# Retention into dropless experts on one core: q scaled ahead of v in two of twelve steps, and the filling counts taken behind the early rows' numbers

## The chip, the cores and the metric

The kernel runs on 1 core of one Trainium2 chip. The metric is device time in microseconds (us) of one launch. Inputs and outputs are float32 in device memory. The core has five engines with a queue of instructions each: TensorE (PE, matrix products), VectorE (DVE), ScalarE (ACT), GpSimd (POOL) and SyncE (SP, which here only starts transfers). They run side by side and wait for each other through semaphores.

## What is computed

Two blocks follow each other. The first is a recurrent retention over 768 positions, for 4 batches and 8 heads of width 64; the second sends each of the 3072 resulting rows (512 wide) to one of 8 experts.

```python
# retention, per batch and head
state = gamma * state + outer(k[t], v[t])
y[t]  = scale * q[t] @ state
# x = y, as 3072 rows of 512
logits = x @ w_gate;  e = argmax(logits);  gate = softmax(logits)[e] / (1 + 1e-9)
out    = gate * (relu(x @ w1[e]) @ w2[e])     # w1[e]: 512x1024, w2[e]: 1024x512
```

Every row goes through exactly one expert, and an expert takes all rows that chose it.

## The kernel before

**Twelve steps of attention.** The recurrence is computed in chunks of 128 positions. A step `s` (0 to 11, `STEPS` is 12) does one chunk for two of the four batches (`b` = 0, 1). `where[s]` is (pair of chunks, pair of batches, which chunk of the pair): steps 8 and 10 begin the last pair of chunks, 9 and 11 end it. For each of its two batches a step does the following:

- `scale_q` (L489) and `scale_v` (L494) multiply q and v by powers of the decay, on POOL. One `scale_v` is one instruction, one `scale_q` is two. The q of two steps are loaded and scaled together, so q of step 10 (as the code counts) serves steps 10 and 11.
- `turn_q` and `turn_k` (L500) transpose q and k on TensorE with an identity into banks of PSUM (`trq`, `trk`), and ACT copies them out.
- `scores` (L532) multiplies k and q into four banks `sc`; DVE masks them (`am`, L536). `with_state` (L555) multiplies q with the old state, `next_state` (L568) makes the new one (`new`) out of k and the scaled v, and DVE adds it to the old one (L574). `within` (L586) multiplies the masked scores with the scaled v, and ACT copies the result `y` out as `x[s]`.
- `logits` (L614, L623) makes the gate's logits of the step before; `to_rows` (L597, DVE) turns its x into rows and `store` (L604, SP) writes them to `x_d` in device memory.

**Where the rows go.** `place(i)` takes the logits of a stretch of steps (0 to 4, 5 to 8, 9 to 11) and numbers the rows of each expert: one-hot `ohs`, ranks by counting products on TensorE (`rk`, L666 to L670), counts per expert in `acc[:, i + 1]`, and through a product `found` (L708) the list `inv` (L712) of which row sits in which place. It is a generator; `WHEN` says at which points of which step its next piece is issued. For the second stretch the last pieces fall into step 10: `found` and then `inv` are issued ahead of `to_rows(9)`, and `next_state(10)` comes behind.

**Early tiles.** After the second stretch the first 256 places of experts 0 and 1 can be fetched before attention ends. `sources` (L184 to L187) makes the row numbers `src_e`, and POOL issues four indirect transfers from `x_d` into `xs` (L173), two for each expert, with the two `scale_v` of step 11 (counted from 0) between them. ACT copies expert 0's rows to `xe` (L768), TensorE transposes them in step 11 (`tre`, L776) between the two halves of `within`, and the first layer of expert 0 (`hp`, L232) follows. `pad_ranks` (L723 to L731) raises the counts of experts 0 and 1 to at least 256, so that later rows take places behind these tiles: TensorE sums the counts of two experts (`tot`, L726), and three small DVE instructions make `pad` and add it to `acc`. Its result is read by `rk` of the last stretch, at 133.53 us.

**What sets the order.** All engines stand under a manual schedule: each runs its instructions in the order in which the code issues them, and SP and POOL likewise. SP issues q, k, v, the rows' stores and the weights in one queue. The lines around the change are these; the first two numbers of a pair in `SCALED` are steps counted from 0:

```python
VALUES = {STEPS - 5: (STEPS - 3, STEPS - 2)}                 # loads: v of 9 and 10 in step 7
SCALED = {STEPS - 4: (STEPS - 4, STEPS - 3), STEPS - 3: (STEPS - 2,), STEPS - 2: ()}
...
if s % 2 and s + 1 < STEPS:
    scale_q(s + 1, 1)
for i in SCALED.get(s, (s,) if 0 < s < STEPS - 1 else ()):
    for b in range(2):
        scale_v(i, b)
if s % 2 == 0 and s + 2 < STEPS:
    scale_q(s + 2, 0)
```

So before, POOL's order from step 8 on is v8, v9, q10 (both batches), v10, two instructions per batch for q and one for v.

**PSUM.** `ps(tag, bufs, name)` hands out banks of a tag in turn. The tag `tr` has two banks, which `trk`, `found`, `tot`, `new`, `rk` and `tre` share; who asks for a bank waits until its last user has read it.

Of the kernel before, what the change touches and what calls it, by code (L numbers as in the profile page):

```python
# [40 lines left out]
def inner(ap, n):  # L41

    dims = [list(d) for d in ap.ap]
    return bass.AP(tensor=ap.tensor, offset=ap.offset, ap=dims + [[0, n]])
# [9 lines left out]
def kernel(  # L54
# [25 lines left out]
    STEPS = NT // 2  # L80
    NEXT = (0, 5, 9, STEPS)
    NR = len(NEXT) - 1
# [7 lines left out]
    def ps(tag, bufs, name):  # L90
        return psum.tile([P, 512], F32, tag=tag, name=name, bufs=bufs)
# [28 lines left out]
    def rt(shape, name, dt=F32):  # L120
        return route.tile(shape, dt, tag=name, name=name)
# [20 lines left out]
    acc = rt([P, NR + 1, E], "acc", BF16)  # L142
# [28 lines left out]
    def gather(xs, idx, tiles, rows=N):  # L171
        for t in tiles:
            nc.gpsimd.indirect_dma_start(  # L173
                out=xs[:, t, :], out_offset=None, in_=x_d[0:rows, :],
                in_offset=bass.IndirectOffsetOnAxis(ap=idx[:, t : t + 1], axis=0), bounds_check=rows - 1,
                oob_is_err=False)
# [3 lines left out]
    def sources(got, name):  # L180
        m = got.shape[2]
        tok, far = rt([P, m], f"tok{name}"), rt([P, m], f"far{name}")
        src = rt([P, m], f"src{name}", U32)
        nc.vector.tensor_scalar(out=far, in0=got[:, 0, :], scalar1=1.0, scalar2=float(FAR), op0=ALU.is_lt, op1=ALU.mult)  # L184
        nc.vector.tensor_tensor(out=far, in0=got[:, 1, :], in1=far, op=ALU.add)
        nc.vector.scalar_tensor_tensor(out=tok, in0=got[:, 0, :], scalar=float(L), in1=far, op0=ALU.mult, op1=ALU.add)
        nc.vector.tensor_scalar(out=src, in0=tok, scalar1=-float(L), scalar2=None, op0=ALU.add)  # L187
        return src, far
# [262 lines left out]
    with ExitStack() as actx:  # L451
# [32 lines left out]
        def scale_q(s, b, by=nc.gpsimd, parts=1):  # L484
            got = raw.pop(("q", s, b))
            qs = raw["qs", s, b] = att.tile([P, 2, H, D], F32, tag="qs", name="qs")
            for part in (ts(i, H // parts) for i in range(parts)):
                for e in range(2):
                    by.tensor_tensor(out=qs[:, e, part, :], in0=got[:, part, ts(e, D)], op=ALU.mult,  # L489
                                     in1=inner(dec[:, ts(2 * where[s][0] + e, H)][:, part], D))  # L490

        def scale_v(s, b, by=nc.gpsimd):
            vs = att.tile([P, H, D], F32, tag="vs", name="vs", bufs=4)
            by.tensor_tensor(out=vs, in0=raw.pop(("v", s, b)), op=ALU.mult,  # L494
                             in1=inner(dec[:, ts(NC + 2 * where[s][0] + where[s][2], H)], D))
            raw["vs", s, b] = vs
# [18 lines left out]
        def turn_k(s, b):  # L515
            kT = att.tile([P, HP, P], F32, tag="kT", name="kT")
            tr = pairs_of("tr", 2, "trk")
            heads_first(raw["k", s, b], tr)
            nc.scalar.copy(out=kT, in_=tr)
            front[s, b] = kT  # L520
# [4 lines left out]
        def scores(s, b):  # L525
            kT, qT = front.pop((s, b)), q_of(s, b)
            sc = [pairs_of("sc", 4, "sc") for _ in range(2)]
            am = [att.tile([P, HP, P], F32, tag=f"am{j}", name=f"am{j}") for j in range(2)]
            for a in range(HP):
                for j in range(2):  # L530
                    r = ts(j, D)
                    nc.tensor.matmul(sc[j][:, a, :], lhsT=kT[r, a, :], rhs=qT[r, a, :], start=True, stop=True)  # L532

            def mask():
                for j in range(2):
                    nc.vector.tensor_tensor(out=am[j], in0=sc[j], in1=middle(causal[:, :], HP), op=ALU.mult)  # L536

            return am, mask
# [3 lines left out]
        def outputs():  # L542
            return [ps("y", 2, "y").rearrange("p (b a t) -> p b a t", b=2, a=HB) for _ in range(2)]
# [86 lines left out]
        def place(i):  # L630
# [82 lines left out]
            if i == NR - 2:  # L713
                head = inv[:, :, 0 : TC + HALF]
                src, far = sources(head, "_e")
                for e in range(2):
                    gather(xs2[e], src[:, e * TC :], range(HALF), 2 * NEXT[i + 1] * P)
                    if e == 0:
                        for b in range(2):
                            scale_v(STEPS - 1, b)  # L720
                early.extend([head, far])

        def pad_ranks(at):  # L723

            tot = ps("tr", 2, "tot")[:, 0:2]
            nc.tensor.matmul(tot, lhsT=ones_b, rhs=at, start=True, stop=True)  # L726
            pad = att.tile([P, 2], F32, tag="pad", name="pad")
            nc.vector.scalar_tensor_tensor(out=pad, in0=inner(row2[:, 0], 2), scalar=float(EARLY), in1=tot,
                                           op0=ALU.add, op1=ALU.subtract)
            nc.vector.tensor_scalar(out=pad, in0=pad, scalar1=0.0, scalar2=2.0, op0=ALU.max, op1=ALU.min)  # L730
            nc.vector.tensor_tensor(out=at, in0=at, in1=pad, op=ALU.add)  # L731

        def load_all(nm, s):
            for b in range(2):
                load(nm, s, b)
# [41 lines left out]
                copies[t](out=xT[:, :, ts(t, P)], in_=tr)  # L777

        VALUES = {STEPS - 5: (STEPS - 3, STEPS - 2)}
        SCALED = {STEPS - 4: (STEPS - 4, STEPS - 3), STEPS - 3: (STEPS - 2,), STEPS - 2: ()}  # L780
        rest = iter(())
        WHEN = {5: "abc", 6: "b", 7: "ab", 8: "pp", 9: "ac", 10: "mpp"}

        def step(s, at):
            for _ in range(WHEN.get(s, "").count(at)):
                next(rest, None)

        for s in range(STEPS):
            if s + 3 < STEPS:
                if s % 2:  # L790
                    load_all("q", s + 3)
                load_all("k", s + 3)
            for i in VALUES.get(s, (s + 2,) if s + 5 < STEPS else ()):
                load_all("v", i)
# [7 lines that stand above are left out]
            if s in (1, 2):  # L802
                nc.gpsimd.memset(xs2[s % 2], 0.0)
            if s:
                am = [scores(s, b) for b in range(2)]
                am[0][1]()
                step(s, "m")
                am[1][1]()
            y = outputs()
            if s + 1 == STEPS:  # L810
                logit = logits(s - 1)
            if where[s][0] or where[s][2]:
                with_state(s, y)

            def ahead():
                for b in range(2):
                    turn_k(s + 1, b)

            def ahead_q():
                if s % 2:  # L820
                    for b in range(2):
                        turn_q(s + 1, b)

            if s:
                if s + 1 < STEPS:
                    logit = logits(s - 1)
                    ahead()
                if s + 1 == STEPS:
                    xe = whole_rows(xs2[0])
                reduce = logits_of(s - 1, *logit)  # L830
                step(s, "p")
                if s + 1 < STEPS:
                    ahead_q()
                to_rows(s - 1)
                reduce()
                if s + 1 == STEPS:
                    wa.append(weights2(first, 0, 2))
                store(s - 1)
                if s == NEXT[NR - 1]:
                    load_all("v", STEPS - 1)  # L840
                    wa = [weights1(first, 0, 2)]
                if s in NEXT:
                    rest = chain(rest, place(NEXT.index(s) - 1))
                step(s, "a")
            next_state(s)
            if s == 0:
                ahead()
            step(s, "b")
            if s == NEXT[NR - 1] + 1:
                pad_ranks(acc[:, NR - 1, 0:2])  # L850
            step(s, "r")
            within(s, y, am, (lambda: early_rows(xe, xTa, (nc.vector.tensor_copy, nc.scalar.copy)))
                   if s + 1 == STEPS else lambda: None)
            step(s, "c")
# [269 lines left out]
```

## Time and profile before

| what | value |
|---|---|
| median of 3 runs | 455.89 us (453.74 to 457.38) |
| the profiled execution's own time | 458.76 us |
| its span, first to last instruction | 456.8 us |
| TensorE busy | 430.3 us, 94% of the span |
| VectorE, POOL, ACT busy | 292.1, 260.5, 131.9 us |
| mean granted TensorE clock | 0.987 of full speed |

The profile is of one execution. Busy times of engines overlap, so they don't add up to the span. "Idle before" a row is the time in which that engine had nothing running, with the event that ended it. Times in the text count from the span's start. Attention takes the first 126 us; the first product of expert 0's first layer starts at 126.13 us, and from there TensorE runs almost without a gap up to the last microseconds.

### The profile page before, as it was taken

What the parts mean: (1) busy time and instruction counts of PE and PEld (TensorE: products, weight loads), DVE (VectorE), ACT (ScalarE), POOL (GpSimd) and SP (SyncE); (2) the same over time, 40 slices, a digit from 0 to 9 for tenths busy, and PEclk for the clock granted to TensorE, in tenths of its full rate; (3) what the DMA queues carried; (4) which work ended last, traced back from release to release, by engine and by line L of the source; (5) the groups of instructions that cost most, each with busy time, mean ns of one, the idle gap of its engine ahead of it and who ended that gap; (6) DMA issues with size and microseconds to landing.
All of it is one profiled execution on the core that took longest, in us unless ns stands there. A gap on an engine that the chain in (4) does not pass through costs nothing.

```text
span 456.8 us, 9680 instructions
## 1 busy us (share of the span) xinstructions
PE 430.3 (94%) x3651; PEld 361.4 (79%) x3651; DVE 292.1 (64%) x600; ACT 131.9 (29%) x298; POOL 260.5 (57%) x216
## 2 busy tenths in 40 slices
PE   6999998969799999999999999999899999999992
PEld 3788887858678868869968985997798689599772
DVE  4454787667868974775776678387677768744410
ACT  2356354334342112310331321124133113202310
POOL 4474544252506978519845890985489189278311
PEclk9999999989899999999999999999999999999997
DMA  8999999999966546644532815172272534001001
GB/s 190 213 236 205 229 205 219 238 214 250 304 187 230 187 120 218 250 187 128 192 99 94 279 53 183 42 292 85 110 249 74 187 101 164 6 5 64 4 29 50
DMA packets 94471, 72.75 MB, mean 159 GB/s; under 512 B 53898, under 2 KB 78474, under 8 KB 94352
## 3 DMA queue, kind: packets, MB, share of 16 engines
q1 hardware_dynamic: 89088, 58.74, 45.9%
q0 software_dynamic: 5120, 12.60, 8.2%
q8 instruction: 47, 0.77, 0.7%
q14 instruction: 72, 0.59, 0.4%
q10 hardware_dynamic: 144, 0.05, 0.0%
HBM read 60.88 MB, written 14.68 MB: 165 GB/s over the span
## 4 chain that ended last, share of the span: by engine, by line
PE 75%; DMA 7%; DVE 7%; issue 4%; SPq 3%; POOL 2%; ACT 1%; POOLq 0%; ACTq 0%; DVEq 0%
PE p L311 27%; PE p L357 17%; PE p L245 13%; DMA q<-in_q_dram 4%; PE hp L232 3%; PE y L586 3%; DMA v<-in_v_dram 3%; SPq L604 2%; PE sc L532 2%; PE p L232 2%; PE new L568 1%; PE y L555 1%; DMA w1t<-in_moe_w_dram 1%; PE yp L357 1%; POOL qs L489 1%
## 5 line engine op out<-in xcount | busy, mean ns | idle before, releaser
L245 PE MATMUL p<-w2t,hT 128*8 128x128 f32 (+6 forms) x496 | 66.4, 360 | 0.0
L245 PEld LDWEIGHTS p<-w2t,hT 128*8 128x8 f32 (+6 forms) x496 | 32.6, 123 | 29.2 <-issue 26.4
L405 POOL DMA_INDIRECT out_dram<-o,dst x30 | 29.9, 995 | 29.1 <-ACT o L253 13.0
L216 DVE STREAM_TRANSPOSE xT<-xs 32x512 f32<-32x512 f32 (+1 forms) x64 | 40.7, 635 | 6.8 <-issue 5.5
L536 DVE TENSOR_TENSOR am<-sc,causal 128x512 f32<-128x512 f32 x48 | 30.0, 683 | 21.0 <-PE sc L532 20.9
L494 POOL TENSOR_TENSOR vs<-v,dec 128x512 f32<-128x512 f32 x23 | 23.7, 1045 | 33.5 <-DMA v<-in_v_dram 33.3
L311 PE MATMUL p<-t,s 128*128 128x196 f32 (+5 forms) x224 | 41.7, 329 | 0.0
L311 PE MATMUL p<-t,w1t 128*128 128x196 f32 (+5 forms) x224 | 41.7, 329 | 0.0
L1083 POOL COPY turn_of<-t 128x1 f32<-128x1 f32 x6 | 1.1, 184 | 70.1 <-DVE t L297 70.1
L315 DVE TENSOR_TENSOR hT<-p,q 128x196 f32<-128x196 f32 (+5 forms) x84 | 28.6, 359 | 16.6 <-PE p L311 16.0
L216 DVE STREAM_TRANSPOSE xTs<-xs 32x512 f32<-32x512 f32 x48 | 33.7, 702 | 7.0 <-issue 6.1
L173 POOL DMA_INDIRECT xs<-x_d,src x28 | 29.6, 1059 | 14.8 <-issue 8.0
L311 PEld LDWEIGHTS p<-t,s 128*128 128x128 f32 x224 | 37.8, 190 | 0.0
L311 PEld LDWEIGHTS p<-t,w1t 128*128 128x128 f32 x224 | 37.8, 190 | 0.0
L357 PE MATMUL p<-ws,hs 128*128 128x256 f32 x168 | 37.4, 379 | 0.0
L315 DVE TENSOR_TENSOR q<-p,q 128x196 f32<-128x196 f32 (+5 forms) x56 | 19.0, 360 | 26.8 <-ACT q L323 13.5
L357 PEld LDWEIGHTS p<-ws,hs 128*128 128x128 f32 x168 | 31.9, 190 | 4.3
L273 POOL TENSOR_TENSOR ws<-w2t,ws 128x1024 f32<-128x1024 f32 x14 | 34.4, 2455 | 0.6
L273 POOL TENSOR_TENSOR ws<-w2t 128x1024 f32<-128x1024 f32 x14 | 33.2, 2369 | 0.1
L489 POOL TENSOR_TENSOR qs<-q,dec 128x512 f32<-128x512 f32 x22 | 22.3, 1042 | 17.0 <-DMA q<-in_q_dram 16.1
L363 DVE SCALAR_TENSOR_TENSOR o<-p,gate,q 128x256 f32<-128x256 f32 x21 | 10.0, 483 | 27.9 <-PE p L357 23.8
L357 PE MATMUL p<-w2t,hT 128*128 128x256 f32 x112 | 26.9, 381 | 0.1
(203 smaller groups left out, 835.1 us busy)
## 6 DMA issues: line engine op xcount, KB each, us to landing
w1t<-in_moe_w_dram SPq DMA_DIRECT2D x7, 2048.0 KB, 8.7
w2t<-in_moe_w_dram SPq DMA_DIRECT2D x7, 2048.0 KB, 9.4
k<-in_k_dram SPq DMA_DIRECT2D x24, 256.0 KB, 5.1
v<-in_v_dram SPq DMA_DIRECT2D x24, 256.0 KB, 5.7
x_d<-xg SPq DMA_DIRECT2D x48, 128.0 KB, 3.9
q<-in_q_dram SPq DMA_DIRECT2D x11, 512.0 KB, 6.1
w1t<-in_moe_w_dram SPq DMA_DIRECT2D x2, 1024.0 KB, 8.6
w2t<-in_moe_w_dram SPq DMA_DIRECT2D x2, 1024.0 KB, 9.8
```

The costliest lines, as they stand in the source:

```text
L173: nc.gpsimd.indirect_dma_start(out=xs[:, t, :], out_offset=None, in_=x_d[0:rows, :], in_offset=bass.IndirectOffsetOnAxis(ap=idx[:, t : t + ...
L216: nc.vector.transpose(xT[ts(g, L), :, 0 : n * P].rearrange("p a (t r i) -> p r t a i", r=Q, i=L)[:, r, :, :, :], xs[ts(r, L), tiles[0] : t ...
L232: nc.tensor.matmul(hp, lhsT=w1t[:, 0, dt, ts(f, P)], rhs=xT[:, dt, 0:n], start=(dt == 0), stop=(dt == DT - 1))
L245: nc.tensor.matmul(y[j * z : j * z + m, 0:c], lhsT=hT[:, f, t * P + r0 : t * P + r0 + m], rhs=w2t[:, 0, f, ts(j, c)], start=(i == 0), stop ...
L273: by.tensor_tensor(out=ws[i], in0=sums[i][0], in1=sums[i][1], op=ALU.subtract)
L311: nc.tensor.matmul(rows(y), lhsT=a(d, f), rhs=b(d), start=start and d == 0, stop=d == 1, skip_group_check=True)
L315: nc.vector.tensor_tensor(out=to, in0=rows(y), in1=rows(plus), op=ALU.add)
L357: nc.tensor.matmul(y, lhsT=a[:, f, :], rhs=b[:, f, :], start=start and f == 0, stop=f == FH - 1, skip_group_check=True)
L405: done = nc.gpsimd.indirect_dma_start(out=out[:, :], out_offset=bass.IndirectOffsetOnAxis(ap=idx[:, t : t + 1], axis=0), in_=o[:, t, :], i ...
L489: by.tensor_tensor(out=qs[:, e, part, :], in0=got[:, part, ts(e, D)], op=ALU.mult, in1=inner(dec[:, ts(2 * where[s][0] + e, H)][:, part], D))
L494: by.tensor_tensor(out=vs, in0=raw.pop(("v", s, b)), op=ALU.mult, in1=inner(dec[:, ts(NC + 2 * where[s][0] + where[s][2], H)], D))
L536: nc.vector.tensor_tensor(out=am[j], in0=sc[j], in1=middle(causal[:, :], HP), op=ALU.mult)
```

## The change

In step 8 POOL scales v of step 8 alone, and v of step 9 moves behind q of step 10, to step 9: POOL's order becomes v8, q10, v9, v10. Counted from one these are the ninth and tenth step. `pad_ranks` is issued inside `place`, behind the early transfers and the two `scale_v` of step 11, instead of behind `next_state(10)`.

```diff
@@ place, for the second stretch
                 for e in range(2):
                     gather(xs2[e], src[:, e * TC :], range(HALF), 2 * NEXT[i + 1] * P)
                     if e == 0:
                         for b in range(2):
                             scale_v(STEPS - 1, b)
+                pad_ranks(acc[:, NR - 1, 0:2])
                 early.extend([head, far])
@@
-        SCALED = {STEPS - 4: (STEPS - 4, STEPS - 3), STEPS - 3: (STEPS - 2,), STEPS - 2: ()}
+        SCALED = {STEPS - 3: (STEPS - 3, STEPS - 2), STEPS - 2: ()}
@@ the loop over steps
             step(s, "b")
-            if s == NEXT[NR - 1] + 1:
-                pad_ranks(acc[:, NR - 1, 0:2])
             step(s, "r")
```

In the compiled program the number of instructions on each engine is the same. On TensorE `tot` goes from behind the 32 products of `new` to ahead of them. On DVE the three instructions of `pad_ranks` go from behind `xg` (two transposes), `lg` and `state` to ahead of them, directly behind `src_e`. On POOL two `vs` go from ahead of four `qs` to behind them. ACT and SP keep their order. As `tot` asks for its bank of `tr` ahead of `new`, `new` gets the bank that `found` held, and in the compiled program its first product then waits for VectorE as well.

## The prediction

> **What bounds the kernel now.** I read the page's slices first, then the waits around the two edits, then the order of time there. TensorE (PE) is busy 94% of the span, and from 126 us on it hardly stops. So what this change can give must come out of the last two steps of attention, 96 to 126 us, and it is worth what it moves the first product of expert 0's first layer (`hp`, L232, 126.13 us) forward.
>
> ```profile
> PE   6999998969799999999999999999899999999992
> PEclk9999999989899999999999999999999999999997
> DMA  8999999999966546644532815172272534001001
> ```
>
> Slices 8 and 10 (91 to 103 and 114 to 126 us) are the only ones ahead of the last where the granted clock dips, and PE has its holes there. DMA is full up to 126 us: transfers set the pace of all that waits for data in this stretch.
>
> ```profile
> 99.78 3.99 PE L500 MATMUL trq<-ident,qs 128*128 128x128 f32 x16 [3.44 <-POOL qs L489]
> 119.52 0.64 PE L614 MATMUL parts<-xT,wg 128*32 128x256 f32 x8 [2.42 <-DVE am L536]
> ```
>
> These are PE's two holes, 5.86 us together. The first ends when POOL has scaled q of step 10 (from 0). POOL's own rows tell why that is late:
>
> ```profile
> 96.65 2.08 POOL L494 TENSOR_TENSOR vs<-v,dec 128x512 f32<-128x512 f32 x2 [10.24 <-DMA v<-in_v_dram]
> 98.69 4.05 POOL L489 TENSOR_TENSOR qs<-q,dec 128x512 f32<-128x512 f32 x4
> 102.69 2.05 POOL L494 TENSOR_TENSOR vs<-v,dec 128x512 f32<-128x512 f32 x2
> ```
>
> POOL stands 10.24 us for v9 with q10 queued behind it, and q10 had landed at 89.8 and 91.7 us (issued at 84.57 and 86.12, median 5.4 to landing). The second hole ends with a mask, and DVE's rows show what held the masks:
>
> ```profile
> 116.17 2.61 DVE L731 TENSOR_TENSOR acc<-acc,pad 128x2 bf16<-128x2 bf16 x1
> 118.70 2.47 DVE L536 TENSOR_TENSOR am<-sc,causal 128x512 f32<-128x512 f32 x4
> ```
>
> Two columns took 2.61 us; the same sum at 106.74 took 0.17. It ends at 118.78, and POOL's two `vs` of step 11 end at 118.74. So a DVE sum of two SBUF operands stood behind POOL's. `scores` were ready at 117.1.
>
> Each hole is paid twice, as the windows show (length, PE busy with its count, the other engines, clock, DMA):
>
> ```profile
> 96.69:100.10 3.41, 0.32 (x3) 0.32 (x4) 3.23 (x6) 0.16 (x1) 3.41 (x4) 1.00 0.93 230
> 100.10:103.51 3.41, 3.27 (x16) 2.29 (x13) 0.71 (x1) 1.84 (x3) 3.41 (x4) 0.50 0.94 224
> 117.17:120.58 3.41, 1.06 (x25) 0.68 (x28) 3.41 (x5) 0.31 (x2) 2.93 (x4) 1.00 0.97 279
> 120.58:123.99 3.41, 3.41 (x42) 2.54 (x34) 2.03 (x4) 1.10 (x3) 0.70 (x1) 0.50 0.93 276
> ```
>
> After a window of 3.41 us with little work, PE runs the next 3.41 us at half clock and loses 1.71. `trq` took 3.99 us for what takes 1.91 at 76.45.
>
> **The order of v and q.** Nothing is added; two `vs` go behind four `qs`. POOL then does q10 from 89.9 (landing) to 92.0 and 92.0 to 94.1, under its old wait. PE's `trq` starts at 96.35 instead of 99.78 and takes 1.75 (chain of waits, full clock) to 98.1. v9 still lands at 96.65, so its `vs` still end at 98.73, then v10 runs to 100.8 (needed by `new` at 108). `within(9)` has 0.25 wait for the second `vs` and ends at 100.1. Next is `rk`, which waits for `ohs` on DVE; `ohs` ends at 100.81 as before, since the DVE chain from 96.96 ran beside POOL work then and does now. PE idles 0.8, `rk` ends at 101.3 (before: 105.94). If the cover of q10 were gone (q landing after v9), the 3.44 would stay.
>
> From there DVE binds: the three gate instructions (0.65) now follow `ohs` at 100.85, `own` starts at 101.55, and after its 1.55 us the masks of step 10 at 103.1, where before they started at 107.60: 4.5 earlier. DVE was full from there to `src_e` (113.82), so `inv` ends at 108.5 and `src_e` at 109.3.
>
> **The counts.** On PE `tot` (0.16) now lies ahead of `new`; harmless itself. But `new` then takes the bank of `found` and waits for `inv`: it starts at 108.6, though PE is through at 107.45 (`found` 111.81 and `tot`, less 4.5). A new wait of 1.15. The queue behind it is `within(10)` and `scores(11)`: `new` 1.10, 1.75, 1.99, so 113.45. On DVE the three `pad` instructions (0.14, 0.17, 0.17 with gaps: 0.6) lie in front of `xg`, `lg`, `state` (2.1), which end at 112.0; the masks of step 11 wait for PE's first eight products (112.5) and not for DVE. POOL's `vs` start at 112.2, long after `acc`. So `parts` runs at 113.45 without a wait, against 119.52: 6.1 earlier. If `acc` is held again, that is a rival below.
>
> **What is late next.** `parts`, `with_state`, the two logit transposes and half of `within` (0.57, 1.03, 0.22, 0.9) end at 116.2. Then `tre` needs `xe`, and that needs the two early transfers of expert 0. POOL issues them 0.29 and 1.85 after `src_e`: 109.6 and 111.15. Stores of rows that they read landed by about 109. Their time to landing:
>
> ```profile
> xs<-x_d,src_e POOLq DMA_INDIRECT x1, 5.1
> ```
>
> ```profile
> xs<-x_d,src_e POOLq DMA_INDIRECT x1, 8.3
> ```
>
> The first is that of 114.11, when most of `w1t` (packets from 110.3 to 117.5) had gone; the second that of 118.91, with all of `w2t` just issued. The four took 5.1, 4.6, 8.3, 8.0. Here a rule speaks: the Trainium skill, page "DMA: Bandwidth & Descriptors", section "Queues, rings and completion order", has each DMA engine go round-robin between queues, packet by packet. By it the transfer needn't wait for the weights: 5.1 and 4.6, landed at 114.7 and 115.8, no wait at `tre`, `hp` at 116.2 + 1.02 + 1.02 = 118.2, a gain of 7.9. By the row of 118.91 the landings are 117.9 and 119.2, `xe` is done at 119.85 (0.6 each), `hp` at 121.5, a gain of 4.6. In the trace the third transfer's packets began only at 123.0, when 269 of `w2t`'s 1024 had started; by then `w1t`, further ahead by 1.2 us, would be at 112.5. I take 1.2 less than the slow row: 7.1 and 6.8, landed at 116.7 and 118.0; `tre` at 117.5 and 118.8 (idle 1.3 and 0.8), then 0.5 and 1.02: `hp` at 120.4. Gain 5.7. Half of `w1t` must have landed (115.95, plus 1.4 for sharing with 0.5 MB): it has.
>
> From `hp` on each transfer is asked for by an instruction that moves along, or has slack (`w2t` landed at 130.35, read at 140.02; expert 1's transfers landed at 128.3, read at 131.24), so the gain reaches the end.
>
> **The sum.** Holes removed 5.86, half clock removed 3.41; new waits 0.25 + 0.8 + 1.15 + 2.1 = 4.3; the remainder to 5.7 (0.7) is rows whose queue gaps I haven't carried. Own time 458.76 becomes 453.1. The runs' median is 2.87 below that execution, and I don't expect all of 5.7 there: the windows above lie on a fixed grid (100.10, 120.58: six times 3.41). The skill's page "TensorE: Matmul & The Clock Gate", "Part 1: The HAM clock gate", calls the window free-running and wants a whole idle window. By that rule the 2.42 hole costs no half clock; the trace has 1.06 of 3.41 busy and half clock after it, so the row decides: somewhere below 2.35 idle is enough. With a threshold of 1.7 to 2.35 and a grid at random, the old holes (3.44, 2.42) cost 1.7 down to 1.0 half-clock windows in a middling run instead of 2: 1.1 us less to win. My new hole at `tre` (2.2 in parts) costs one at most in half of the runs: 0.4. So 5.7 - 1.1 - 0.4 = 4.2, and 455.89 becomes **451.7**.
>
> **Rivals.**
> - *The early transfers land in time* (fast row, 7.9 - 1.1 = 6.8): **449.0**. For it: the round-robin rule; against: the slow rows.
> - *They come late and PE falls to half clock at `tre`* (4.6 - 1.1 - 1.3): **453.7**; behind all of `w1t` (119.5 and 120.2) about 455.
> - *`acc` is held again.* It now runs at 109.8, while POOL issues the first early transfer (109.6 to 110.85); before it started inside one too (115.67 to 116.68) and 0.5 ahead of the `vs`. Held to the end of `vs` (114.3), the masks start at 116.5, `parts` at 117.2, with a hole of 3.7 and its half clock: 2.3 - 1.1, **454.7**. Against: two-operand sums at 164.74 beside a transfer of 164.60 took the usual 0.69. From both sides 0 to 4.4 us for DVE; I take 0, by that row.
> - *Slower:* the early transfers, now started ahead of the weights' flow and not at its end, wait for both loads, 4 MB. At 0.37 MB/us from 110.4 that is 121.3; landing after 123.8 the gain is gone, and only after 128 is it over 1% lost: about **460**. No transfer here took over 11.1 us.
>
> **Chances.** 451.7: 0.43; in time: 0.22; late: 0.18; `acc` held: 0.11; slower: 0.06. A measurement of this kernel can tell about 1% (4.56 us: below 451.33). The middle case lies just above and has about 0.4 of its chance below it; with nearly all of the second that gives faster 0.38, same 0.56, slower 0.06. The likeliest case alone is 450.4 to 453.2. The range leaves out the slower case and the far end of the others: 448.2 to 455.6.
>
> **What would show it.** `trq` without idle ahead of it and near 1.9 us; `rk` with a short wait on `ohs`; `new` waiting for DVE; `acc` at 0.17; no half clock at either old place; then an idle at `tre` with ACT's `xe` behind a DMA, and `hp` near 120.4. Wrong if `acc` stays long, if `hp` gains and the later rows give it back, or if `tre` waits beyond 122.

## The result, and the profile after

| what | before | after |
|---|---|---|
| median | 454.72 us (22 runs, 452.26 to 460.53) | 450.80 us (22 runs, 448.47 to 457.34) |
| the profiled execution's own time | 458.76 us | 450.67 us |
| its span | 456.8 us | 448.9 us |
| mean granted TensorE clock | 0.987 | 0.991 |

The ratio is 0.9906, with a 95% interval of 0.9885 to 0.9927: 3.9 us less at the median, about 1%. (The 22 runs of the kernel before contain the three of the table further up.) Some executions of every kernel are several us longer than its others; the ratios leave the disturbed ones out.

The granted clock of the changed kernel, in 40 slices of the span:

```profile
PEclk9999999999899999999999999999999999999997
```

Of the two dips of the clock one is gone, that of slice 8, and the second, in slice 10, now lies at 112 to 123 us. PE's rows from the transposes of q to the first layer of expert 0 (start, us, engine, line, what, and in brackets the idle time before it and what ended it):

```profile
94.33 1.91 PE L500 MATMUL trq<-ident,qs 128*128 128x128 f32 x16
98.38 0.20 PE L666 MATMUL rk<-ohs,before 128*128 128x64 bf16 x1 [0.24 <-DVE ohs L648]
...
104.51 0.17 PE L727 MATMUL tot<-acc,ones_b 128*128 128x2 bf16 x1
105.94 1.15 PE L568 MATMUL new<-vs,k 128*64 128x64 f32 x32 [1.26 <-DVE inv L712]
...
110.81 0.64 PE L614 MATMUL parts<-xT,wg 128*32 128x256 f32 x8
...
115.37 0.66 PE L777 MATMUL tre<-ident,xe 128*128 128x128 f32 x4 [1.49 <-ACT xe L769]
116.40 0.87 PE L777 MATMUL tre<-ident,xe 128*128 128x128 f32 x4 [0.37 <-ACT xe L769]
...
119.10 1.62 PE L232 MATMUL hp<-xTa,w1t 128*128 128x256 f32 x4
```

Both old holes are gone: `trq` has no idle ahead of it and takes 1.91 us instead of 3.99, and `parts` no longer waits. In their place stand four short waits: 0.24 at `rk`, 1.26 at `new`, and 1.49 and 0.37 at `tre`. To compare times, one shift is needed. `new` of step 7, ahead of everything that was edited, starts at 78.64 us here and at 80.48 in the profile before. So this execution was 1.84 us ahead already, and I add 1.84 to its times where they are set against those of before. `hp` then stands at 120.94 against 126.13, 5.2 us earlier.

POOL's rows show the new order, and ACT's rows what `tre` waits for:

```profile
88.16 4.05 POOL L489 TENSOR_TENSOR qs<-q,dec 128x512 f32<-128x512 f32 x4 [3.41 <-DMA q<-in_q_dram]
94.15 4.10 POOL L494 TENSOR_TENSOR vs<-v,dec 128x512 f32<-128x512 f32 x4 [1.94 <-DMA v<-in_v_dram]
...
106.90 1.25 POOL L173 DMA_INDIRECT xs<-x_d,src_e  x1 [6.36 <-DVE pad L731]
108.45 1.02 POOL L173 DMA_INDIRECT xs<-x_d,src_e  x1 [0.30 <-DMA v<-in_v_dram]
109.49 2.04 POOL L494 TENSOR_TENSOR vs<-v,dec 128x512 f32<-128x512 f32 x2
```

```profile
114.69 0.62 ACT L769 COPY xe<-xs 128x512 f32<-128x512 f32 x1 [2.77 <-DMA xs<-x_d,src_e]
115.72 0.62 ACT L769 COPY xe<-xs 128x512 f32<-128x512 f32 x1 [0.41 <-DMA xs<-x_d,src_e]
```

q is scaled while v9 is still on its way. The two early transfers are issued at 106.90 and 108.45, and ACT stands until each has landed. Their time to landing, in the rows of DMA issues (one row for each):

```profile
xs<-x_d,src_e POOLq DMA_INDIRECT x1, 7.7
...
xs<-x_d,src_e POOLq DMA_INDIRECT x1, 7.3
```

DVE's rows show that `acc` is no longer held:

```profile
106.44 0.17 DVE L187 TENSOR_SCALAR src_e<-tok_e 128x6 uint32<-128x6 f32 x1
...
106.91 0.19 DVE L732 TENSOR_TENSOR acc<-acc,pad 128x2 bf16<-128x2 bf16 x1
...
109.97 2.48 DVE L536 TENSOR_TENSOR am<-sc,causal 128x512 f32<-128x512 f32 x4 [0.84 <-PE sc L532]
```

It takes 0.19 us instead of 2.61, and the masks behind it now wait for PE and not PE for them. Last the windows of PE's clock around `tre` (length, PE, weight loads, DVE, ACT, POOL, clock, DMA):

```profile
109.88:113.29 3.41, 3.41 (x70) 2.52 (x68) 3.32 (x6) 0.55 (x2) 2.94 (x4) 1.00 1.00 341
113.29:116.70 3.41, 1.54 (x19) 1.07 (x16) 1.12 (x4) 1.59 (x3) 0.76 (x1) 1.00 1.03 359
116.70:120.12 3.42, 3.42 (x23) 2.58 (x22) 1.26 (x11) 1.60 (x4) 0.00 (x0) 0.50 1.05 391
```

The wait at `tre` is paid as the old holes were: PE was busy for 1.54 of 3.41 us, and the next 3.42 us ran at half clock.

### The profile page after: what moved, and what is told of

The parts are those of the page before. It is cut to its first block, busy times and chain, and to the rows that moved or that the text cites. A ratio compares the mean times of both kernels' runs of the same rounds, so it can differ in the third digit from the quotient of the medians.

```text
span 448.9 us, 9682 instructions
## 1 busy us (share of the span) xinstructions
PE 428.7 (96%) x3651; PEld 361.2 (80%) x3651; DVE 286.7 (64%) x600; ACT 131.7 (29%) x298; POOL 260.4 (58%) x216
## 4 chain that ended last, share of the span: by engine, by line
PE 77%; DMA 7%; DVE 6%; issue 4%; SPq 1%; POOL 1%; ACT 1%; POOLq 0%; ACTq 0%; DVEq 0%
PE p L311 28%; PE p L357 17%; PE p L245 13%; PE y L586 4%; PE sc L532 4%; DMA v<-in_v_dram 2%; PE new L568 2%; PE p L232 2%; DMA xs<-x_d,src_e 2%; PE y L555 2%; PE trk L500 2%; PE hp L232 2%; DVE xTa L216 1%; DMA q<-in_q_dram 1%; PE trq L500 1%
```

## The experiments

The theory: each edit removes its own hole, but both only move the same next limit forward, the landing of expert 0's two early transfers, and so the gains of the edits overlap. Rivals: the gains add, and what is missing is lost at the new wait of `new` on `inv`; `acc` was held by POOL's transfers and not by its `vs`; the transfers are slow because of the weights that are asked for ahead of them. Ratios are to the kernel before, run on the same chip. What "earlier" or "later" means between two profiled executions is counted from `src_e`, since `src_e` lies up to 5 us apart in them.

**The order of v and q alone**, in the kernel before.

```diff
-        SCALED = {STEPS - 4: (STEPS - 4, STEPS - 3), STEPS - 3: (STEPS - 2,), STEPS - 2: ()}
+        SCALED = {STEPS - 3: (STEPS - 3, STEPS - 2), STEPS - 2: ()}
```

> Of the two edits, the order of v and q alone; the counts stay where they were. My theory (the gain is cut by the early transfers at tre, so the two edits overlap): 0.991 to 0.993 of before, nearly what both gave (0.9906); trq without idle, src_e about 4.5 us earlier than before, new without a wait for DVE, but acc is held beside the two vs of step 11 once more (about 2.5 us) and PE has a hole of 2 to 3 us ahead of parts; then tre waits little, as the early transfers have landed meanwhile. Rival (the two gains add, each with its own hole): 0.995 to 0.996, that is 5.9 times 3.4 of the 5.9 us of holes.

Ratio 0.9888 (0.983 to 0.9946), median 451.47 us. PE's row for `tre`, DVE's for `acc` and POOL's for the `vs` behind the transfers:

```profile
113.09 0.66 PE L776 MATMUL tre<-ident,xe 128*128 128x128 f32 x4 [0.47 <-ACT xe L768]
116.11 1.12 PE L776 MATMUL tre<-ident,xe 128*128 128x128 f32 x4 [2.36 <-ACT xe L768]
```

```profile
108.64 0.16 DVE L731 TENSOR_TENSOR acc<-acc,pad 128x2 bf16<-128x2 bf16 x1
```

```profile
109.43 2.04 POOL L494 TENSOR_TENSOR vs<-v,dec 128x512 f32<-128x512 f32 x2
```

This edit alone gives as much as the whole change. That `acc` would be held was a miss: it took 0.16 us, with `vs` starting 0.79 us after it (in the profile before, 0.52). So the second hole went away without the second edit, `parts` ran at 109.55, 3.43 us behind `src_e` (106.12), where the changed kernel has 4.37, and it brought nothing: the second `tre` starts 9.99 us behind `src_e`, in the changed kernel 9.96. PE waits 2.36 us for a transfer. What reached the limit earlier only waits longer there. The ratio lies below the expected 0.991 to 0.993, but its interval covers them.

**The counts alone.** The changed kernel with the old `SCALED` line.

```diff
-        SCALED = {STEPS - 3: (STEPS - 3, STEPS - 2), STEPS - 2: ()}
+        SCALED = {STEPS - 4: (STEPS - 4, STEPS - 3), STEPS - 3: (STEPS - 2,), STEPS - 2: ()}
```

> Of the two edits, the earlier counts alone; q10 stays behind v9. My theory: trq keeps its wait for POOL (about 3.4 us) and its half clock; acc takes about 0.2 us, the hole ahead of parts (2.4 us) and its half clock go, new waits for inv about 1.2 us, and parts comes about 1.4 us earlier; with the half clock that fell into some of the runs, 0.995 to 0.997 of before. Rival (the new wait of new takes back what acc gives): 0.999 to 1.001.

Ratio 0.9961 (0.9933 to 0.9988), median 453.87 us. PE's rows, of an execution of 459.25 us in which PE also stood 4.70 us for DVE in the expert phase, later than all that is shown here:

```profile
96.80 4.12 PE L500 MATMUL trq<-ident,qs 128*128 128x128 f32 x16 [2.80 <-POOL qs L489]
...
111.37 1.15 PE L568 MATMUL new<-vs,k 128*64 128x64 f32 x32 [1.27 <-DVE inv L712]
116.23 0.64 PE L614 MATMUL parts<-xT,wg 128*32 128x256 f32 x8
...
119.23 1.09 PE L777 MATMUL tre<-ident,xe 128*128 128x128 f32 x8
```

The first hole is there with its half clock (`trq` takes 4.12), the hole ahead of `parts` is gone, the wait of 1.27 us at `new` has come, and `tre` doesn't wait. The transfers, issued at 112.33 and 113.88, took 3.8 and 4.3 us: the weights asked for ahead of them, by 106 us, were as good as in (their last packets at 112.5). If gains added, 0.9888 and 0.9961 would make 0.985; the change has 0.9906. The interval of the first is too wide to show this by the ratios alone; the rows at `tre` show it.

**What held `acc`.** In the kernel before, all four early transfers go ahead of the two `vs` of step 11.

```diff
                 for e in range(2):
                     gather(xs2[e], src[:, e * TC :], range(HALF), 2 * NEXT[i + 1] * P)
-                    if e == 0:
-                        for b in range(2):
-                            scale_v(STEPS - 1, b)
+                for b in range(2):
+                    scale_v(STEPS - 1, b)
```

> The kernel before, with the two scale_v of step 11 issued behind all four early transfers and not between the second and the third. acc then starts as before, half a microsecond into or behind the second transfer, but no vs follows at once. My theory (POOL's two-operand vs hold DVE's sum): acc takes about 0.2 us, the masks of step 11 start when scores are ready, and PE's hole of 2.4 us ahead of parts shrinks to under 0.5. Rival (the indirect transfer on POOL holds it, and it would hold acc in the changed kernel too in some executions): acc takes 1 us or more and the hole stays over 1 us.

One run: 454.63 us. DVE's row and POOL's:

```profile
114.20 0.16 DVE L730 TENSOR_TENSOR acc<-acc,pad 128x2 bf16<-128x2 bf16 x1
```

```profile
113.70 1.01 POOL L173 DMA_INDIRECT xs<-x_d,src_e  x1 [0.30 <-issue]
```

`acc` starts 0.50 us into the issue of the second transfer, just as in the profile before (116.17 and 115.67), and isn't held. What differs is what POOL does next, a third transfer and no `vs`. So it was the `vs`. The hole ahead of `parts` is gone, but the late `vs` (from 117.36) now make `within` wait, 1.31 and 0.33 us.

**The kernel before again**, unchanged, one execution.

> The kernel before once more, for a second look at acc. If the hold depends on how close POOL's vs of step 11 follow (0.52 us behind acc's start in the first profile, 0.79 without a hold in the kernel with q's order alone), acc may take 0.2 or 2.6 us here, and parts goes with it; trq waits about 3.4 us for POOL in either case.

455.77 us. DVE's row and POOL's, then the windows of both holes:

```profile
114.81 2.62 DVE L731 TENSOR_TENSOR acc<-acc,pad 128x2 bf16<-128x2 bf16 x1
```

```profile
115.35 2.04 POOL L494 TENSOR_TENSOR vs<-v,dec 128x512 f32<-128x512 f32 x2
```

```profile
95.82:99.23 3.41, 0.83 (x6) 0.59 (x7) 3.13 (x5) 0.47 (x1) 3.36 (x5) 1.00 0.94 233
99.23:102.64 3.41, 3.41 (x18) 2.39 (x19) 0.00 (x0) 1.83 (x4) 3.41 (x4) 0.50 1.07 261
...
116.30:119.71 3.41, 1.54 (x40) 1.05 (x40) 3.41 (x5) 0.79 (x2) 2.95 (x4) 1.00 1.03 266
119.71:123.12 3.41, 3.41 (x50) 2.77 (x42) 2.61 (x10) 1.80 (x4) 0.21 (x1) 1.00 1.01 341
```

The hold is no accident of one execution: 2.62 us, again with `vs` 0.54 us behind its start. The hole ahead of `parts` is 2.42 us here as before, but this time no half clock follows it. The grid of windows lies otherwise, and the same hole is shared out between two of them.

**Is the new wait at `new` on the path?** First try: `tot` goes into unused columns of `found`'s bank, so that `new` gets another.

```diff
-            found = ps("tr", 2, "found")[:, 0 : 5 * E * TC]
+            bank = ps("tr", 2, "found")
+            found = bank[:, 0 : 5 * E * TC]
...
-                pad_ranks(acc[:, NR - 1, 0:2])
+                pad_ranks(acc[:, NR - 1, 0:2], bank[:, 256:258])
```

> The changed kernel with tot in spare columns of the bank of found, so that new gets the bank that it had before and needn't wait for inv. My theory (the end of attention is set by the early transfers, whose issue depends on DVE alone): new's wait of 1.26 us goes, the idle ahead of tre grows by the same, hp stays where it is, and the time is that of the changed kernel, 0.989 to 0.992 of before. Rival (the new wait is on the path): 1.2 us less, 0.988 of before, and hp 1.2 us earlier against src_e.

Ratio 0.9918 (0.9891 to 0.9944). PE's row shows why this tells nothing:

```profile
103.90 0.16 PE L727 MATMUL found<-acc,ones_b 128*128 128x2 bf16 x1 [1.18 <-DVE inv L713]
```

The wait moved from `new` to `tot` itself, which now lies in the bank that `inv` reads. Second try: `tot` in a bank of the scores.

```diff
-            tot = ps("tr", 2, "tot")[:, 0:2]
+            tot = ps("sc", 4, "tot")[:, 0:2]
```

> The changed kernel with tot in a bank of the tag sc and nothing else, so that new really doesn't wait for inv (in the bank of found the product tot waited for it instead). My theory: parts comes 1.2 us earlier against src_e, the idle ahead of tre grows by 1.2, hp and the time stay: 0.989 to 0.992 of before. Rival (the new wait is on the path): 1.2 us less than the changed kernel, about 0.988.

Ratio 0.9939 (0.9913 to 0.9965). PE's rows:

```profile
102.38 1.15 PE L568 MATMUL new<-vs,k 128*64 128x64 f32 x32
107.65 0.64 PE L614 MATMUL parts<-xT,wg 128*32 128x256 f32 x8
...
112.31 0.66 PE L777 MATMUL tre<-ident,xe 128*128 128x128 f32 x4 [1.59 <-ACT xe L769]
113.98 0.66 PE L777 MATMUL tre<-ident,xe 128*128 128x128 f32 x4 [1.02 <-ACT xe L769]
```

Now the wait is gone: `parts` comes 3.43 us behind `src_e` (104.22), 0.94 nearer than in the changed kernel. PE waits 2.61 us at `tre` instead of 1.86, and the second `tre` starts 9.76 us behind `src_e`, almost where it did with the wait (9.96). No time is gained: the ratio is above the expected 0.989 to 0.992, with an interval that reaches into it. `hp` does come nearer to `src_e`, 11.37 us instead of 12.66, but that is the half clock, which is missing in this execution. So the wait of 1.26 us at `new` is covered by the wait for the transfers, and the rival that puts the loss there falls.

**The changed kernel again**, on the same chip as the last.

> The changed kernel once more, on the same chip as the three below, to compare them with it. 0.9906 of before, as measured.

Ratio 0.9892 (0.9844 to 0.994), median 451.52 us, in agreement with 0.9906. In the profiled execution (456.62 us) `tre` waits 1.96 and 0.33 us, its second row starts 10.38 us behind `src_e`, the transfers take 8.2 and 7.7, and half clock follows (116.86 to 120.27).

**The weights in the transfers' way.** The second half of expert 0's first weights (its fetch waits in the list `w1_later`) goes behind the store of step 10's turn.

```diff
                 store(s - 1)
+                if s == NEXT[NR - 1] + 1:
+                    w1_later.pop()()
                 if s == NEXT[NR - 1]:
                     load_all("v", STEPS - 1)
-                    wa = [weights1(first, 0, 2)]
+                    wa = [weights1(first, 0, 2, w1_later)]
```

> The changed kernel with the second half of expert 0's w1 (1 MB) asked for behind the rows' store of step 10 and not ahead of it, so that only 1 MB of weights lies in the queue when the early transfers start. It is read first about 8 us after the first product of the layer, so it has time. My theory (transfers that flow among the weights set hp): expert 0's early transfers land in about 5 us after their issue and not 7.7 and 7.3, ACT's xe waits under 0.5 us for them, tre has no idle ahead of it (1.86 us before), the half clock there goes, and hp comes about 2 to 3 us earlier against src_e: 0.984 to 0.987 of before. Rival (PE's and DVE's own chain sets hp, the wait at tre only fills slack): 0.990 to 0.991. If the transfers' time does not depend on the weights in the queue, it stays at 7 us and so does the time.

Ratio 0.9903 (0.9873 to 0.9933). A miss: the transfers weren't shorter, but took 8.4 and 7.4 us. (Here and in the next three runs, the landing of the first transfer is taken from the start of ACT's copy.) The half was only moved from 106 to about 110 us and went into the same stretch, with `w2t` right behind it. PE's row, a wait of 2.22 us in one piece:

```profile
114.91 1.18 PE L782 MATMUL tre<-ident,xe 128*128 128x128 f32 x8 [2.22 <-ACT xe L774]
```

Together with `tot` in a bank of the scores:

> The kernel with the half of w1 later, and tot in a bank of the tag sc, so that new needn't wait for inv. My theory: with the transfers out of the way new's wait of 1.26 us is on the path, at least until the transfers bind again: 0.3 to 1.2 us less than with the later half of w1 alone, 0.982 to 0.986 of before. Rival (the transfers still set hp): the same time as with the later half alone.

Ratio 0.988 (0.9844 to 0.9916), above the expected 0.982 to 0.986 and not to be told from the 0.9903 without `tot` in that bank; the transfers took 7.2 and 6.6 us, `tre` waits 1.92 and 0.29. Nothing that the changed kernel doesn't have.

Then that half and all of `w2t` behind the store of the last step's turn, at 118.9 us and later, so that during the transfers only 1 MB of weights is asked for, not 4:

```diff
-                if s + 1 == STEPS:
-                    wa.append(weights2(first, 0, 2))
                 store(s - 1)
-                if s == NEXT[NR - 1] + 1:
+                if s + 1 == STEPS:
                     w1_later.pop()()
+                    wa.append(weights2(first, 0, 2))
```

> The changed kernel with the second half of expert 0's w1 and all of its w2 (3 MB) asked for behind the rows' store of step 11's turn, so that during expert 0's early transfers only 1 MB of weights, v and one store of rows lie in the queue. With the half of w1 alone the 1 MB was followed at once by the store, the other half and w2, and the transfers took as long as ever. My theory, in its second form (the transfers share the engines with all that is queued while they are under way, not only with what was ahead of them): they land 4 to 5.5 us after their issue, tre waits under 0.7 us, hp starts about 9.5 us behind src_e's start and not 12.5, and the time is 2 to 3 us under the changed kernel's, 0.983 to 0.987 of before; the second half of w1 lands ahead of its use by a microsecond or two. Rival (the time to landing is what an indirect transfer takes, 7 us whatever lies beside it): no difference to the changed kernel. A third outcome: the late w1 half stops hp at its fifth product, and the gain is lost there.

Ratio 0.9878 (0.984 to 0.9915). PE's rows:

```profile
116.57 0.66 PE L782 MATMUL tre<-ident,xe 128*128 128x128 f32 x4 [0.36 <-ACT xe L774]
117.80 0.66 PE L782 MATMUL tre<-ident,xe 128*128 128x128 f32 x4 [0.58 <-ACT xe L774]
119.41 1.13 PE L237 MATMUL hp<-xTa,w1t 128*128 128x256 f32 x4
```

The transfers took 6.6 and 6.3 us, about 1 less than in the changed kernel, PE waits 0.94 us, half as long, and `hp` follows 10.63 us behind `src_e`. The time can't be told from that of the changed kernel, and transfers, wait and `hp` all miss the forecast. The gain on the transfers is hardly more than what executions differ by: in the changed kernel and in its variants with all weights in place they took from 6.9 to 8.2 us. Nor does the run show what they take without weights, as 1 MB of `w1t`, v and the rows still kept the DMA engines full. The packets say more. These are the queues' rows of the changed kernel from 110.9 and from 111.2 us (0.3 us each; packets, MB, share of the 16 engines; `q0` has POOL's transfers, `q1` SP's):

```profile
q1 hardware_dynamic: 59, 0.12, 103.8%
...
q1 hardware_dynamic: 51, 0.10, 90.7%
q0 software_dynamic: 1, 0.00, 3.3%
```

And these are of the run with the counts alone, where `w1t` was in, from 113.9 and from 114.2 us:

```profile
DMA packets 0, 0.00 MB, mean 0 GB/s; under 512 B 0, under 2 KB 0, under 8 KB 0
...
q0 software_dynamic: 9, 0.04, 107.2%
```

With idle DMA engines the first packet moves 2.0 us behind the start of the issue and the transfer lands after 3.8. In the changed kernel, with the engines full of SP's transfers, the first packet moves only after 4.5 us and the landing comes at 7.7. So 2.5 of the 3.9 us more pass before the first packet, though POOL's issue takes 1.25 us in both; with 3 MB of weights taken away the first packet comes after 3.1. The same with `tot` in a bank of the scores, the combination that the theory favours:

> The kernel with the weights behind the rows, and tot in a bank of the tag sc. If the transfers land in 4 to 5.5 us, new's wait of 1.26 us comes onto the path in part: up to 1 us less than with the weights behind the rows alone, 0.981 to 0.986 of before. If tre still waits for the transfers, the same time as without.

Ratio 0.9864 (0.9829 to 0.99), the lowest of all, but its interval overlaps that of the changed kernel; the transfers took 7.1 and 6.5 us, `tre` waits 1.84 and 0.22, and half clock follows. No version here is shown to beat the changed kernel.

**The half clock behind `tre`.** Two products whose result nobody reads are put ahead of `tre`, to keep PE busy while it waits.

```diff
         def early_rows(xe, xT, copies):
+            for _ in range(2 if xT is xTa else 0):
+                warm(512)
             for t in range(HALF):
```

> The changed kernel with two products of idle data (128x512) issued ahead of the eight tre transposes, where PE otherwise idles 1.86 us in two parts. They add work and nothing to the result. If the half clock behind that idle (116.70 to 120.12) comes from the idle, the clock stays whole there, and the time is 0 to 1.7 us less, on average about 0.5: 0.988 to 0.991 of before. If PE's own chain were the limit there, they would cost their own 1.7 us: 0.994.

Ratio 0.9899 (0.9861 to 0.9938). PE's rows:

```profile
115.14 0.66 PE L779 MATMUL tre<-ident,xe 128*128 128x128 f32 x4
116.15 0.66 PE L779 MATMUL tre<-ident,xe 128*128 128x128 f32 x4 [0.35 <-ACT xe L769]
117.76 1.13 PE L232 MATMUL hp<-xTa,w1t 128*128 128x256 f32 x4
```

No half clock came, though the transfers were late as before, and `hp` follows 11.9 us behind `src_e` (105.85), against 12.7 in the changed kernel. The time doesn't show 0.8 us. That fits what the prediction assumed, that half clock at `tre` comes in some executions only: among the profiled executions with the order of q changed and without filler it came behind `tre` in five (both of the changed kernel, q alone, and two of the variants above) and not in four. So one execution without half clock doesn't yet show that the two products kept it away.

## Why the prediction was right

The forecast was 451.7 us, 4.2 less than before; measured were 450.8 and 3.9 less. Its steps, with 1.84 added to the times of the changed kernel:

| step | predicted | measured |
|---|---|---|
| `trq` starts, takes | 96.35, 1.75 | 96.17, 1.91 |
| wait of `rk`, its end | 0.8, 101.3 | 0.24, 100.6 |
| `src_e` ends | 109.3 | 108.45 |
| wait of `new` on `inv` | 1.15 | 1.26 |
| `parts` | 113.45 | 112.65 |
| transfers to landing | 7.1, 6.8 | 7.7, 7.3 |
| waits at `tre` | 1.3, 0.8 | 1.49, 0.37 |
| `hp` | 120.4 | 120.9 |

**The order of v and q** did what was said: no wait, no half clock. PE then met DVE at `rk`, as predicted, with one term mis-sized. "The DVE chain ran beside POOL work then and does now" took over the old durations; but `dl`, a sum of two SBUF operands, took 0.82 us before and 0.23 after, though `vs` run beside it in both (before, then after):

```profile
96.96 0.82 DVE L642 TENSOR_TENSOR dl<-lg,mx 128x64 f32<-128x64 f32 x1
```

```profile
95.11 0.23 DVE L642 TENSOR_TENSOR dl<-lg,mx 128x64 f32<-128x64 f32 x1
```

That is most of the 0.65 us by which `ohs` ends earlier.

**The counts** did what was said too: `acc` 0.19, `parts` without a wait, a new wait at `new` within 0.11 us of the forecast. Its sum lists this wait as a loss of 1.15. It is none of its own: without it PE waits at `tre` instead, as the prediction's own chain has it, where the landing sets `tre`. That sum also doesn't close: 5.86 + 3.41 - 4.3 is 4.97, and the 0.7 up to 5.7 was put down to gaps that weren't counted. (Among the rivals, 455.89 less 6.8 is 449.1, not 449.0.)

**What is late next** was named rightly, the early transfers, and their time was mis-sized by 0.5 to 0.6 us. They were issued 0.86 us earlier than predicted, since `ohs` and what follows it came earlier, and so landed within 0.5 us of the forecast: two errors that cancelled by luck. `tre` was then through sooner than predicted, and `hp` is nonetheless 0.5 us late because of the half clock: PE ran 2.4 us of it before `hp`, so 1.2 us were lost there. Of the two rows that the prediction weighed, that of the longer transfers was nearer. By the rule of the Trainium skill (page "DMA: Bandwidth & Descriptors", section "Queues, rings and completion order": each DMA engine takes turns between its queues, packet by packet) the transfers would have taken about 5 us and left no wait. They took 7.3 to 8.2 us in both executions of the changed kernel, 5.5 and 7.1 with the order of q alone, 3.8 and 4.3 where the weights ahead of them were nearly all in, and 6.3 to 7.1 with 3 MB of weights taken away. So the rule's direction holds: when the first packet moved, 616 of the 1024 packets of `w1t` had started, so it wasn't put behind all that was asked for earlier. But the rule doesn't give the time. The 2.5 us that pass before the first packet, and the slower flow behind it, make up the difference; why the first packet waits so long behind full engines stays open, as what each of the 16 engines still had in its queue was not seen.

**From `hp` to the end** the gain held: 330.67 us before, 329.80 after. The 0.87 us more come from the expert phase, where one wait of a second-layer product for DVE was 1.7 us before and is 0.4 after, less about 0.5 of half clock that is still to come at `hp`. Whether the change has to do with that wait wasn't tried.

**The rivals.** "`acc` is held again" fell, by the row above and by the run with the transfers first; "in time" fell by the wait at `tre`; "slower" by the landing after 7 to 8 us. "Late, with half clock at `tre`" was seen in the profiled execution as to the half clock, but the transfers landed at 116.4 and 117.6 and not at the 117.9 and 119.2 that it was worked out from.

**The clock.** The prediction took 1.1 us off for holes that fall badly or well on a grid of 3.41 us. The kernel before, run again, shows just that: same two holes, one half clock instead of two. On the page "TensorE: Matmul & The Clock Gate", "Part 1: The HAM clock gate", the window is said to be free-running, which this agrees with, and half clock to follow an idle window; here it followed windows with 0.83 and 1.54 us of work. The prediction put the threshold at 1.7 to 2.35 us of idle time. The two windows with 1.87 us idle lie in that band; one was followed by half clock (the changed kernel) and one was not (the kernel before run again). The other profiles narrow the band. Cut into windows on the grid that each shows, from 20 us on up to 8 us ahead of the end, all fourteen together have 11 windows at full clock with at most 1.49 us of PE work, and half clock followed every one; it followed none with 1.67 us or more; and of five between 1.54 and 1.60 it followed three. So in these runs the border lies between 1.74 and 1.92 us of idle time in one window, and a hole is paid for when so much of it falls into a single window.

## What to carry to other kernels

When two holes on the way to the same transfer are closed, cost them against its landing and not one by one: here one edit gave 1.1% (0.5 to 1.7%), the other 0.4%, and both together 0.9%, and the rows at `tre` showed why. Before an instruction that waits is put down as a loss, see what its engine waits for next: 1.26 us at `new` cost nothing that the runs could show, since the same time would have been spent at `tre`. And a transfer that is moved earlier has to be timed among the transfers that it now meets; by its old rows (5.1 and 4.6 us) it would have been put 2.6 us too early.

## What was not expected of the hardware

- By the times of the profile, a small DVE sum of two SBUF operands was held to the end of two POOL multiplications that started after it. It was held, for 2.61 and 2.62 us, where they started 0.52 and 0.54 us after it; it took 0.16 where they started 0.79 us after it, and 0.16 inside the issue of an indirect transfer. The Trainium skill ("GPSIMD Engine Reference", "8. Key points") names contention of POOL with DVE instructions that have two SBUF inputs; that one which has already started can be held is what these rows add. Where between 0.54 and 0.79 us it ends wasn't measured.
- The same 256 KB by an indirect transfer took from 3.8 us (the weights ahead of it nearly all in) to 8.4 us (weights around it). Moving 1 MB of the weights back by some 4 us changed nothing (8.4 and 7.4); moving 3 MB behind the transfers gave at most about 1 us. Most of the difference lies ahead of the first packet, which moved 2.0 us behind the start of the issue with idle DMA engines and 4.5 us behind it with full ones.
- Half clock also came far from any edit, behind waits in the expert phase. In the run with `tot` in a bank of the scores PE stood 5.14 us for DVE, up to 319.60, and the clock was halved from 316.91 to 323.74; in the changed kernel run again it stood 4.72 us, up to 153.19, and the clock was halved from 150.99 to 157.82. That is two windows each time, as the wait reached over two windows in a row and left little work in each (0.96 and 0.72 us, 0.89 and 1.21). In the first profile of the changed kernel the wait at the second place is 0.33 us, and no half clock follows.
